# A grouped-query attention block with a K/V cache: part of wo on four DMA engines, sums on VectorE, and division after the turn to tokens

## The chip, the cores and the metric

The kernel runs on one core of one Trainium2 chip. The metric is device microseconds of one execution. Before the change the runs took 187.44, 187.71 and 189.12 us, median 187.71. One execution was also recorded by the hardware profiler: 187.35 us, with a span of 185.6 us from its first to its last instruction.

## The reference

B = 8 sequences with 4 new tokens each, D = 512, 32 query heads, 8 K/V heads (4 query heads share one), 2048 cached keys, head size 128, all bf16.

```python
q = (x @ wq).reshape(B, Sq, Hq, Dh).transpose(0, 2, 1, 3)
k = jnp.repeat(k_cache, rep, axis=1)
v = jnp.repeat(v_cache, rep, axis=1)
scores = jnp.einsum("bhqd,bhkd->bhqk", q, k) * (Dh ** -0.5)
p = softmax(scores, axis=-1)
o = jnp.einsum("bhqk,bhkd->bhqd", p, v)
return o.transpose(0, 2, 1, 3).reshape(B, Sq, Hq * Dh) @ wo
```

k_cache and v_cache are 33.6 MB each, wq and wo 4.2 MB each: 75.5 MB are read for 32 KB of output.

## The kernel before, in words

The work is cut into 16 units: one sequence b and four of the eight K/V heads (a half hq). A unit has one K tile and one V tile of 2 MB, 128 rows of 16 KB (four heads by 32 stretches of 64 keys). Three K and three V tiles fit (`KB, VB`). The main loop (L327) runs n = 1 to 17: in step n TensorE turns unit n's K, makes unit n-1's scores and unit n-2's V products. Inside a step the order is written out by hand, and each engine runs its instructions in this order; semaphores between engines follow from the tiles.

- `transpose_part` (L144): a quarter of a K tile. TensorE turns eight 128 x 128 blocks (two bf16 taken as one fp32), four to a PSUM buffer `kp` of one bank out of three; VectorE (DVE) copies each four to `kt` (L155).
- `scores` (L213): 16 matmuls into two `s_ps` buffers; ScalarE (ACT) takes the exponential of each into `s_sb` and adds up the rows on the way (`accum_out`, L230).
- `probs_to_keys` (L237): TensorE turns the exponentials so that keys are in rows (`pt`, one PSUM buffer); ACT copies them in eight copies of 32 x 512 to `probs` (L249), one of two buffers.
- `norms` (L256): the row sums are spread by a product on DVE (L258), added over the four groups of rows by a matmul with ones (L265), and DVE takes the reciprocal (L273). Once a unit.
- `values` (L277): 64 matmuls add V's products into `o_ps` (one PSUM buffer); `finish` (L290): DVE multiplies by the reciprocals and writes `oT` in bf16.
- `to_tokens`, `to_wo_rows` (L299, L307): after the eight units of a half, TensorE turns `oT` so that the 64 rows are tokens, DVE copies, TensorE turns again so that rows are rows of wo, DVE copies to `oP`.
- `project` (L316): 16 matmuls for each quarter p of wo's rows, two for each r, into `out_ps`. Quarter 0 stands in step 17 ahead of the last unit's V products, quarters 1 to 3 at the end.

At the start come K0, wq and x, the turn of K0, and q, which is laid out in `q_bd` by DVE and ACT in turn (L202).

All loads are issued by SyncE (SP), in one order: K0, wq, x, K1, K2, V0, K3, V1 and so on, K15, V13, quarter 0 of wo, V14, V15, then quarters 1, 2, and 3 in two parts (6 and 2 of the 8 r's), then four small loads of x into `spare`, of 5, 7, 1 and 3 rows. A load waits for its buffer, and for the load eight before it, since eight semaphores are used in turn. The two stores are issued by ACT and SP.

Of the kernel before, what the change touches and what calls it, by code (L numbers as in the profile page):

```python
# [14 lines left out]
def kernel(  # L15
# [35 lines left out]

    const = ctx.enter_context(tc.tile_pool(name="const", bufs=1))
# [5 lines left out]
    psum_k = ctx.enter_context(tc.tile_pool(name="psum_k", bufs=3, space=bass.MemoryType.PSUM))  # L58
# [3 lines left out]
    psum_l = ctx.enter_context(tc.tile_pool(name="psum_l", bufs=1, space=bass.MemoryType.PSUM))  # L62
# [6 lines left out]
    probs = [const.tile([128, C, G, HQ], BF16, name=f"probs{i}") for i in range(2)]  # L69
    ident = const.tile([128, 128], BF16, name="ident")  # L70
    ident4 = const.tile([128, 128], FP32, name="ident4")
    ones = const.tile([128, 128], FP32, name="ones")
    by_hq = const.tile([128, 2, HQ], FP32, name="by_hq")
    oT = [const.tile([128, HP, 2, B, Sq], BF16, name=f"oT{n}") for n in range(2)]
# [3 lines left out]
    spare = const.tile([16, 4, 32], BF16, name="spare")  # L78
# [5 lines left out]

    def load_k(u):
        hq, b = units[u]
        ks[u] = kpool.tile([128, C, Dh], BF16, tag="k_sb", name="k_sb")
        nc.sync.dma_start(
            ks[u][:, :, :],
            k_cache[b, G * hq : G * hq + G].rearrange("g (s c) d -> (g s) c d", c=C),  # L90
        )

    def load_v(u):
        hq, b = units[u]
        vs[u] = vpool.tile([128, C, Dh], BF16, tag="v_sb", name="v_sb")
        rows = v_cache[b, G * hq : G * hq + G].rearrange("g (s c) d -> (g s) c d", c=C)
        nc.sync.dma_start(vs[u][:, :, :], rows)

    def load_wo(p, r0, n):
        rows = wo[p * HP * 128 : (p + 1) * HP * 128, :].rearrange("(q r) j -> q r j", r=WR)  # L100
        nc.sync.dma_start(wo_sb[:, p, r0 : r0 + n, :], rows[:, r0 : r0 + n, :])  # L101

    load_k(0)
# [3 lines left out]
    for u in range(2, NU + 2):  # L107
        if u < NU:
            loads.append(("k", u))
        if u == NU:  # L110
            loads.append(("w", 0))
        loads.append(("v", u - 2))
    loads.reverse()

    def load_ready(nk, nv):

        while loads:
            kind, u = loads[-1]
            if kind == "w":
                load_wo(u, 0, WR)  # L120
            elif u >= (nk + KB if kind == "k" else nv + VB):
                return
            else:
                (load_k if kind == "k" else load_v)(u)
            loads.pop()
# [6 lines left out]
    nc.gpsimd.memset(probs[0][:, :, :, :], 0.0)  # L132
    nc.gpsimd.memset(probs[1][:, :, :, :], 0.0)  # L133
    nc.gpsimd.memset(ones[:, :], 1.0)
    nc.vector.tensor_reduce(
        out=by_hq[:, :, :],
        in_=ident4[:, :].rearrange("p (z c q) -> p z q c", z=2, q=HQ),
        axis=AX,
        op=ADD,
# [4 lines left out]
    def transpose_part(u, t):  # L144
# [4 lines left out]
        for half in range(2):  # L149
            j0 = t % 2 * J + half * J // 2  # L150
            kp = psum_k.tile([128, J // 2, 128], FP32, tag="k", name="kp")
            for j in range(J // 2):
                w = (t * J + half * J // 2 + j) * 128
                nc.tensor.transpose(kp[:, j, :], k4[:, w : w + 128], ident4[:, :])  # L154
            nc.vector.tensor_copy(  # L155
                out=kt[(u, t // 2)][:, j0 : j0 + J // 2, :, :].rearrange("k j s e -> k (j s e)"),
                in_=kp[:, :, :].rearrange("k j s -> k (j s)").bitcast(BF16),
            )
# [52 lines left out]
    l_sbs = {}  # L211

    def scores(u):  # L213
# [3 lines left out]
        l_sbs[u] = small.tile([128, 2], FP32, tag="l_sb", name="l_sb")  # L217
        for y in range(2):
            s_ps = psum_s.tile([128, 2 * J, S], FP32, tag="s", name="s_ps")
            for e in range(2):  # L220
# [13 lines left out]
                accum_out=l_sbs[u][:, y : y + 1],  # L234
            )

    def probs_to_keys(u):  # L237
# [7 lines left out]
        pr = probs[u % 2][:, :, :, :].rearrange("s (x i k w) g q -> s x g i k w q", x=2, k=4, w=2)  # L245
        for x in range(2):
            for g in range(G):
                z, y = g // 2, g % 2
                nc.scalar.copy(  # L249
                    out=pr[g * S : (g + 1) * S, x, g, :, :, :, :],  # L250
                    in_=halves[(2 * x + y) * S : (2 * x + y + 1) * S, z, :, :, :, :],
                )

    r_sbs = {}

    def norms(u):  # L256
        by_gq = small.tile([128, 2, 2, HQ], FP32, tag="by_gq", name="by_gq")
        nc.vector.tensor_tensor(  # L258
            out=by_gq[:, :, :, :],
            in0=l_sbs[u][:, :].unsqueeze(1).unsqueeze(3).to_broadcast([128, 2, 2, HQ]),  # L260
            in1=by_hq[:, :, :].unsqueeze(2).to_broadcast([128, 2, 2, HQ]),
            op=MULT,
        )
        l_ps = psum_l.tile([128, NQ], FP32, tag="l", name="l_ps")
        nc.tensor.matmul(  # L265
            l_ps[:, :],
            lhsT=ones[:, :],
            rhs=by_gq[:, :, :, :].rearrange("k z y q -> k (z y q)"),
            start=True,
            stop=True,  # L270
        )
        r_sbs[u] = small.tile([128, NQ], FP32, tag="r_sb", name="r_sb")
        nc.vector.reciprocal(r_sbs[u][:, :], l_ps[:, :])  # L273
# [3 lines left out]
    def values(u, half):  # L277
        if half == 0:
            o_pss[u] = psum_o.tile([128, NQ], FP32, tag="o", name="o_ps")
        for i in range(half * C // 2, (half + 1) * C // 2):  # L280
# [4 lines left out]
                rhs=probs[u % 2][:, i, :, :].rearrange("s g q -> s (g q)"),  # L285
# [4 lines left out]
    def finish(u):  # L290
        hq, b = units[u]
        nc.vector.tensor_tensor(  # L292
            out=oT[hq][:, :, :, b, :].rearrange("d h p s -> d p h s"),
            in0=o_pss[u][:, :].rearrange("d (p h s) -> d p h s", p=2, h=HP),
            in1=r_sbs[u][:, :].rearrange("d (p h s) -> d p h s", p=2, h=HP),
            op=MULT,
        )

    def to_tokens(n):  # L299
        nat = psum_l.tile([2 * T, HP, 128], BF16, tag="l", name="nat")  # L300
        for h in range(HP):
            nc.tensor.transpose(
                nat[:, h, :], oT[n][:, h, :, :, :].rearrange("d p b s -> d (p b s)"), ident[:, :]
            )
        nc.vector.tensor_copy(out=nat_sb[:, :], in_=nat[:, :, :].rearrange("t h d -> t (h d)"))

    def to_wo_rows(n):  # L307
        perm = psum_l.tile([128, WR, 2, T], BF16, tag="l", name="perm")
        by_row = nat_sb[:, :].rearrange("t (q r) -> t r q", r=WR)
        for r in range(WR):  # L310
            nc.tensor.transpose(
                perm[:, r, :, :].rearrange("q p t -> q (p t)"), by_row[:, r, :], ident[: 2 * T, : 2 * T]
            )
        nc.vector.tensor_copy(out=oP[n][:, :, :, :], in_=perm[:, :, :, :])

    def project(p, r0, n):  # L316
        for r in range(r0, r0 + n):
            for half in range(2):
                nc.tensor.matmul(  # L319
                    out_ps[half * T : (half + 1) * T, :],  # L320
                    lhsT=oP[p // 2][:, r, p % 2, :],
                    rhs=wo_sb[:, p, r, half * DH : (half + 1) * DH],
                    start=(p == 0 and r == 0),
                    stop=(p == NP - 1 and r == WR - 1),
                )

    for n in range(1, NU + 2):  # L327
# [7 lines left out]
        if w >= 0:  # L335
            norms(w)
        if n < NU:
            transpose_part(n, 2)
        if n == NU - 1:
            probs_to_keys(n - 1)  # L340
        if n == NU + 1:
# [65 lines left out]
```

## Time and profile before

| | |
|---|---|
| runs | 187.44, 187.71, 189.12 us |
| profiled execution | 187.35 us, span 185.6 us |
| TensorE (PE) busy | 137.2 us, 74% |
| VectorE (DVE) busy | 103.6 us, 56% |
| ScalarE (ACT) busy | 102.2 us, 55% |
| DMA | 75.86 MB, mean 409 GB/s over the span |
| chain that ended last | DMA 68%, PE 22%, DVE 4% |
| K and V loads | 16 of 2048 KB each; from issue to landing 21.6 and 25.1 us in the median |

How to read it: the page lists busy time of each engine, the span in 40 slices with the busy share in tenths, the DMA queues, the chain of work that ended last, and the groups of instructions by source line, with the mean of one in ns and the idle time before them. In the time-ordered list each row has its start and its length in us from the span's start, the engine, the line, the operation, the output and input tiles, the count of instructions merged in the row, and in square brackets the idle time before it and what ended that. In a row by stretches, the four pairs are busy us and instruction counts of PE, PEld (weight loads), DVE and ACT, then POOL, then the granted clock, the DMA share and GB/s.

### The profile page before, as it was taken

Reading aid. Unit: us, or ns where it says so; the run is one execution under the profiler, and the core shown is the slowest. Engines: PE = TensorE matmul, PEld = TensorE weight load, DVE = VectorE, ACT = ScalarE, POOL = GpSimd, SP = SyncE. Lnnn points to the kernel's source line nnn. Section 1 sums busy time; section 2 is a strip of 40 time slices with the busy share of each in tenths; the row PEclk is TensorE's granted clock in tenths of the full one; section 3 lists DMA queues with packets and bytes.
Section 4 is the critical chain, followed back from the end, with each engine's and each line's share of the span. In section 5 each row is a group of like instructions: output and inputs, shape, how many; then the busy total and the mean of one; then the engine's idle time right before and its main releaser. Section 6 shows DMA issues by size and latency. Waiting matters only on the chain.

```text
span 185.6 us, 4659 instructions
## 1 busy us (share of the span) xinstructions
PE 137.2 (74%) x2036; PEld 113.4 (61%) x2036; DVE 103.6 (56%) x189; ACT 102.2 (55%) x200; POOL 8.2 (4%) x11
## 2 busy tenths in 40 slices
PE   0092869797978777777777869579777777795872
PEld 0192347595866665757575849377666757585651
DVE  4074188777765747475665756466747475661220
ACT  2000153969576666574839292927566574878700
POOL 8900000000000000000000000000000000000000
PEclk9999589999999999999999999999999999999999
DMA  6998999999999999999999999999999999999970
GB/s 187 484 438 378 434 424 431 434 420 431 438 422 431 422 438 410 441 431 424 434 427 431 434 417 431 441 413 438 424 434 434 417 443 420 417 443 411 417 297 8
DMA packets 5668, 75.86 MB, mean 409 GB/s; under 512 B 688, under 2 KB 784, under 8 KB 1040
## 3 DMA queue, kind: packets, MB, share of 16 engines
q1 hardware_dynamic: 5600, 75.55, 95.9%
q8 instruction: 16, 0.26, 0.5%
q14 instruction: 4, 0.03, 0.0%
q10 hardware_dynamic: 48, 0.02, 0.0%
HBM read 75.53 MB, written 0.03 MB: 407 GB/s over the span
## 4 chain that ended last, share of the span: by engine, by line
DMA 68%; PE 22%; DVE 4%; issue 1%; ACT 1%; SPq 1%
DMA k_sb<-in_k_cache_dram 46%; DMA wo_sb<-in_wo_dram 13%; PE kp L154 12%; DMA x_sb<-in_x_dram 9%; DVE kt L155 3%; PE s_ps L223 3%; PE o_ps L282 3%; PE psq L177 2%; PE l_ps L265 1%; ACT q_bd L202 1%; PE out_ps L319 1%; SPq L101 0%; PE pt L242 0%; DVE by_gq L258 0%; DVE q_bd L202 0%
## 5 line engine op out<-in xcount | busy, mean ns | idle before, releaser
L155 DVE COPY kt<-kp 128x1024 bf16<-128x1024 bf16 x128 | 82.0, 683 | 42.7 <-PE kp L154 42.7
L249 ACT COPY probs<-pt 32x512 bf16<-32x512 bf16 x128 | 73.7, 576 | 49.5 <-PE pt L242 46.7
L154 PE MATMUL kp<-ident,k_sb 128*128 128x128 f32 x512 | 70.6, 284 | 20.2 <-DMA k_sb<-in_k_cache_dram 11.2
L154 PEld LDWEIGHTS kp<-ident,k_sb 128*128 128x128 f32 x512 | 58.3, 147 | 28.8 <-DVE oT L292 9.7
L282 PE MATMUL o_ps<-probs,v_sb 128*128 128x64 bf16 x1024 | 34.8, 194 | 0.2 <-DMA v_sb<-in_v_cache_dram 0.2
L282 PEld LDWEIGHTS <-v_sb 128*128 128x128 bf16 x1024 | 33.9, 98 | 0.8 <-DMA v_sb<-in_v_cache_dram 0.5
L230 ACT ACTIVATE s_sb<-s_ps 128x512 bf16<-128x512 f32 x32 | 22.6, 734 | 1.3 <-PE s_ps L223 0.9
L265 PE MATMUL l_ps<-by_gq,ones 128*128 128x64 f32 x32 | 6.9, 298 | 15.6 <-DVE by_gq L258 15.6
L223 PE MATMUL s_ps<-kt,q_bd 128*32 128x512 bf16 x256 | 17.5, 390 | 0.0
L265 PEld LDWEIGHTS l_ps<-by_gq,ones 128*128 128x128 f32 x32 | 4.8, 188 | 19.5 <-DVE by_gq L258 17.7
L273 DVE RECIPROCAL r_sb<-l_ps 128x64 f32<-128x64 f32 x16 | 8.9, 558 | 9.1 <-PE l_ps L265 9.1
L186 ACT ACTIVATE q_nat<-psq 128x512 bf16<-128x512 f32 x2 | 1.2, 597 | 20.4 <-PE psq L177 20.4
L242 PE MATMUL pt<-ident,s_sb 128*128 128x128 f32 x64 | 9.7, 274 | 2.1 <-ACT s_sb L230 2.1
L292 DVE TENSOR_TENSOR oT<-o_ps,r_sb 128x64 bf16<-128x64 f32 x16 | 3.6, 225 | 13.6 <-PE o_ps L282 13.5
L223 PEld LDWEIGHTS <-q_bd 128*32 128x32 bf16 x256 | 5.6, 94 | 6.1 <-issue 2.5
L242 PEld LDWEIGHTS pt<-ident,s_sb 128*128 128x128 f32 x64 | 7.4, 141 | 2.3 <-ACT s_sb L230 2.3
L230 ACT ACTIVATION_READ_ACCUMULATOR s_sb<-s_ps 128x1 f32 x32 | 6.0, 188 | 0.0
L319 PE MATMUL out_ps<-wo_sb,oP 128*32 128x256 bf16 x64 | 4.2, 273 | 1.1 <-DMA wo_sb<-in_wo_dram 0.6
L374 ACT CAST out_sb<-out_ps 64x256 bf16<-64x256 f32 x1 | 0.4, 365 | 6.9 <-PE out_ps L319 6.9
L319 PEld LDWEIGHTS <-oP 128*32 128x32 bf16 x64 | 3.0, 96 | 1.7 <-issue 0.7
L177 PE MATMUL psq<-wq_sb,xT_sb 128*32 128x512 bf16 x32 | 3.6, 631 | 0.3 <-DVE xT_sb L170 0.3
L133 POOL MEMSET probs<- 128x4096 bf16 x1 | 3.5, 3512 | 0.0
(27 smaller groups left out, 29.9 us busy)
## 6 DMA issues: line engine op xcount, KB each, us to landing
k_sb<-in_k_cache_dram SPq DMA_DIRECT2D x16, 2048.0 KB, 21.6
v_sb<-in_v_cache_dram SPq DMA_DIRECT2D x16, 2048.0 KB, 25.1
wq_sb<-in_wq_dram SPq DMA_DIRECT2D x1, 4096.0 KB
wo_sb<-in_wo_dram SPq DMA_DIRECT2D x3, 1024.0 KB, 20.9
wo_sb<-in_wo_dram SPq DMA_DIRECT2D x1, 768.0 KB, 23.2
wo_sb<-in_wo_dram SPq DMA_DIRECT2D x1, 256.0 KB, 23.4
x_sb<-in_x_dram SPq DMA_DIRECT2D x1, 32.0 KB
spare<-in_x_dram SPq DMA_DIRECT2D x1, 0.3 KB
```

Source lines behind the costliest of these rows:

```text
L154: nc.tensor.transpose(kp[:, j, :], k4[:, w : w + 128], ident4[:, :])
L155: nc.vector.tensor_copy(out=kt[(u, t // 2)][:, j0 : j0 + J // 2, :, :].rearrange("k j s e -> k (j s e)"), in_=kp[:, :, :].rearrange("k j s ...
L177: nc.tensor.matmul(psq[g * T : (g + 1) * T, :], lhsT=xT_sb[:, r, :], rhs=wq_sb[:, r, c0 : c0 + rep * Dh], start=(r == 0), stop=(r == R - 1),)
L223: nc.tensor.matmul(s_ps[m * 32 : (m + 1) * 32, :, :], lhsT=q_bd[:, hq, e, g, b, :, :], rhs=kt[(u, th)][:, :, g * S : (g + 1) * S, e], star ...
L230: nc.scalar.activation(out=s_sbs[u][:, :, y, :, :].rearrange("r j s w -> r j w s"), in_=s_ps[:, :, :].rearrange("r (j w) s -> r j w s", w= ...
L242: nc.tensor.transpose(pt[:, i, :], s4[:, i * 128 : (i + 1) * 128], ident4[:, :])
L249: nc.scalar.copy(out=pr[g * S : (g + 1) * S, x, g, :, :, :, :], in_=halves[(2 * x + y) * S : (2 * x + y + 1) * S, z, :, :, :, :],)
L265: nc.tensor.matmul(l_ps[:, :], lhsT=ones[:, :], rhs=by_gq[:, :, :, :].rearrange("k z y q -> k (z y q)"), start=True, stop=True,)
L273: nc.vector.reciprocal(r_sbs[u][:, :], l_ps[:, :])
L282: nc.tensor.matmul(o_pss[u][:, :], lhsT=vs[u][:, 2 * (th * 2 * J + 2 * (2 * j + x) + w) + c, :], rhs=probs[u % 2][:, i, :, :].rearrange("s ...
L292: nc.vector.tensor_tensor(out=oT[hq][:, :, :, b, :].rearrange("d h p s -> d p h s"), in0=o_pss[u][:, :].rearrange("d (p h s) -> d p h s", ...
L319: nc.tensor.matmul(out_ps[half * T : (half + 1) * T, :], lhsT=oP[p // 2][:, r, p % 2, :], rhs=wo_sb[:, p, r, half * DH : (half + 1) * DH], ...
```

## The change

- **wo.** The first 128 rows of quarters 0 and 1 (256 rows) go to a tile `wo_e` of 48 partitions (rows 0 to 15 and 32 to 47 filled, the rest zero) by eight loads of four rows of 8 KB each, which stand after V2 to V9 in the order of loads. The other 896 rows of both quarters come in one load after V15, with seven r's instead of eight, then quarter 2, then quarter 3 in two equal parts. Quarter 0 no longer stands ahead of V14. The `spare` loads are gone. Loads and stores together are 48 (45 before).
- **Projection.** All of it stands at the end: 16 matmuls for `wo_e`, 14 for each of quarters 0 and 1, then 16 for each of quarters 2 and 3; before, 16 stood ahead of the last V products and 48 behind.
- **Sums.** ACT's exponentials add up nothing; DVE adds each unit's `s_sb` (1024 columns) by one reduction into `l_sb` (`add_up`). Once in a half, `sums` spreads them (two products on POOL), adds them by two small matmuls and takes 64 x 8 reciprocals.
- **Division.** `finish` copies `o_ps` to `oT` in fp32; the division is made in `to_tokens`, with tokens in rows, four heads at a time: four steps in all, two in each half, the turned outputs in a `kp` buffer. The small results (`l_ps`, `perm`) use the buffer of the V products; the pool `psum_l` is gone. In the first half these steps are spread over n = 10 to 13.
- **K.** `kp` has two banks and two buffers: eight blocks are turned, then DVE copies 128 x 2048 in one instruction.
- **probs.** Four buffers instead of two (half a unit each); of a unit's eight copies DVE makes the first one (even units) or two (odd units), ACT the rest, group by group.

The core of the diff:

```diff
-    psum_k = ctx.enter_context(tc.tile_pool(name="psum_k", bufs=3, space=bass.MemoryType.PSUM))
+    psum_k = ctx.enter_context(tc.tile_pool(name="psum_k", bufs=2, space=bass.MemoryType.PSUM))
...
-    psum_l = ctx.enter_context(tc.tile_pool(name="psum_l", bufs=1, space=bass.MemoryType.PSUM))
...
+    def load_wo_e(i):
+
+        p0, k0 = i // 4 * 32 + i % 4, i // 4 * HP * 128
+        rows = wo[k0 : k0 + 16 * WR, :].rearrange("(q r) j -> q r j", r=WR)
+        nc.sync.dma_start(wo_e[p0 : p0 + 13 : 4, :, :], rows[i % 4 : i % 4 + 13 : 4, :, :])
...
+    nc.gpsimd.memset(wo_e[:, :, :], 0.0)
     load_k(0)
...
-        if u == NU:
-            loads.append(("w", 0))
         loads.append(("v", u - 2))
+        if 4 <= u < 12:
+            loads.append(("e", u - 4))
...
-        for half in range(2):
-            j0 = t % 2 * J + half * J // 2
-            kp = psum_k.tile([128, J // 2, 128], FP32, tag="k", name="kp")
...
+        kp = psum_k.tile([128, J, 128], FP32, tag="k", name="kp")
+        for j in range(J):
+            w = (t * J + j) * 128
+            nc.tensor.transpose(kp[:, j, :], k4[:, w : w + 128], ident4[:, :])
...
-                accum_out=l_sbs[u][:, y : y + 1],
-            )
+            )
+
+    def add_up(u):
+        hq, b = units[u]
+        nc.vector.tensor_reduce(
+            out=l_sb[hq][:, b, :],
+            in_=s_sbs[u][:, :, :, :, :].rearrange("r j y s w -> r y j (s w)"),
+            axis=mybir.AxisListType.XY,
+            op=ADD,
+        )
...
+        for g in range(G):
+            for x in range(2):
+                pr = probs[u % 2 * 2 + x][:, :, :, :].rearrange("s (i k w) g q -> s g i k w q", k=4, w=2)
                 z, y = g // 2, g % 2
-                nc.scalar.copy(
-                    out=pr[g * S : (g + 1) * S, x, g, :, :, :, :],
+                (nc.vector.tensor_copy if g == 0 and x <= u % 2 else nc.scalar.copy)(
+                    out=pr[g * S : (g + 1) * S, g, :, :, :, :],
                     in_=halves[(2 * x + y) * S : (2 * x + y + 1) * S, z, :, :, :, :],
                 )
...
+        add_up(u)
...
     def finish(u):
         hq, b = units[u]
+        nc.vector.tensor_copy(
+            out=oT[hq][:, :, :, b, :].rearrange("d h p s -> d p h s"),
+            in_=o_pss[u][:, :].rearrange("d (p h s) -> d p h s", p=2, h=HP),
+        )
...
+    def sums(n):
+
+        by_tok = small.tile([128, 2, 2, B, Sq], FP32, tag="by_tok", name="by_tok")
...
+        l_ps = psum_o.tile([2 * T, 2, rep], FP32, tag="o", name="l_ps")
...
+    def to_tokens(n, h0):
+        nat = psum_k.tile([2 * T, 4, 128], FP32, tag="k", name="nat")
...
         nc.vector.tensor_tensor(
+            out=nat_sb[:, h0 * 128 : (h0 + 4) * 128].rearrange("t (h d) -> t h d", h=4),
+            in0=nat[:, :, :],
+            in1=r_sbs[n][:, h0 : h0 + 4].unsqueeze(2).to_broadcast([2 * T, 4, 128]),
             op=MULT,
         )
...
         if w == B:
-            to_tokens(0)
-        if w == B + 1:
+            sums(0)
+        if w in (B, B + 1):
+            to_tokens(0, (w - B) * 4)
+        if w == B + 2:
             to_wo_rows(0)
+        if w == B + 3:
+            to_extra_rows()
         load_ready(min(n + 1, NU), max(w + 1, 0))
...
-            for p, r0, k in [(1, 0, 8), (2, 0, 8), (3, 0, 6), (3, 6, 2)]:
-                load_wo(p, r0, k)
-            for i, k in enumerate([5, 7, 1, 3]):
-                nc.sync.dma_start(spare[:k, i, :], x.flatten_outer_dims()[:k, :32])
-
-    to_tokens(1)
-    project(1, 0, WR)
-    to_wo_rows(1)
-    project(2, 0, WR)
-    for r in range(0, WR, 2):
-        project(3, r, 2)
+            load_wo(0, 0, WM)
+            load_wo(2, 0, WR)
+            for r in (0, 4):
+                load_wo(3, r, 4)
+
+    out_ps = psum_s.tile([2 * T, DH], FP32, tag="s", name="out_ps")
+    sums(1)
+    to_tokens(1, 0)
+    to_tokens(1, 4)
+    for r in range(WR):
+        project(wo_e[:, r], oE[:, r, :], first=r == 0)
+    for p in range(NP):
+        if p == 2:
+            to_wo_rows(1)
+        for r in range(WM if p < 2 else WR):
+            project(wo_sb[:, p, r], oP[p // 2][:, r, p % 2, :], last=p == NP - 1 and r == WR - 1)
```

## The prediction

> **What bounds the kernel now.** I read the page first (which resource is full), then the stretches of the steady part (how full), then the time-ordered list of instructions from the last K tile to the end (which wait ends last there), then the trace's own packet and semaphore records for the sixteen DMA engines. Page and stretches:
>
> ```profile
> span 185.6 us, 4659 instructions
> ...
> DMA  6998999999999999999999999999999999999970
> ...
> q8 instruction: 16, 0.26, 0.5%
> ...
> L155 DVE COPY kt<-kp 128x1024 bf16<-128x1024 bf16 x128 | 82.0, 683 | 42.7 <-PE kp L154 42.7
> L249 ACT COPY probs<-pt 32x512 bf16<-32x512 bf16 x128 | 73.7, 576 | 49.5 <-PE pt L242 46.7
> ```
>
> ```profile
> 60.00:80.00 20.00, 15.84 (x249) 12.97 (x241) 12.41 (x23) 12.93 (x26) 0.00 (x0) 1.00 1.01 431
> 140.00:157.00 17.00, 12.99 (x212) 11.40 (x210) 10.62 (x20) 9.79 (x21) 0.00 (x0) 1.00 1.01 428
> ```
>
> The DMA engines are full from the third slice to the last but one; at 431 GB/s a 2 MB tile takes 4.87 us, a unit (K and V) 9.73, a 1 MB part of wo 2.43. No compute engine is full. The end is another stage; in the time-ordered list:
>
> ```profile
> 154.71 0.60 PE L242 MATMUL pt<-ident,s_sb 128*128 128x128 f32 x4
> 155.40 4.78 ACT L249 COPY probs<-pt 32x512 bf16<-32x512 bf16 x8 [3.56 <-PE pt L242]
> 157.23 1.06 PE L154 MATMUL kp<-ident,k_sb 128*128 128x128 f32 x8 [0.98 <-DMA k_sb<-in_k_cache_dram]
> 160.21 0.73 ACT L230 ACTIVATE s_sb<-s_ps 128x512 bf16<-128x512 f32 x1
> ```
>
> ```profile
> 163.22 4.78 ACT L249 COPY probs<-pt 32x512 bf16<-32x512 bf16 x8 [1.57 <-PE pt L242]
> ...
> 168.03 0.73 ACT L230 ACTIVATE s_sb<-s_ps 128x512 bf16<-128x512 f32 x1
> ...
> 170.28 4.78 ACT L249 COPY probs<-pt 32x512 bf16<-32x512 bf16 x8 [0.80 <-PE pt L242]
> ...
> 174.14 2.06 PE L282 MATMUL o_ps<-probs,v_sb 128*128 128x64 bf16 x64 [0.22 <-DMA v_sb<-in_v_cache_dram]
> 176.24 0.23 DVE L292 TENSOR_TENSOR oT<-o_ps,r_sb 128x64 bf16<-128x64 f32 x1 [2.71 <-PE o_ps L282]
> ...
> 178.79 0.42 DVE L314 COPY oP<-perm 128x512 bf16<-128x512 bf16 x1 [0.92 <-PE perm L311]
> ...
> 180.89 1.05 PE L319 MATMUL out_ps<-wo_sb,oP 128*32 128x256 bf16 x16 [0.56 <-DMA wo_sb<-in_wo_dram]
> 181.97 0.36 ACT L374 CAST out_sb<-out_ps 64x256 bf16<-64x256 f32 x1 [6.92 <-PE out_ps L319]
> ```
>
> From 155.4 ScalarE runs copies, exponentials, copies without rest to 175.06; at 174.14 the last V tile lets the last V products start; at 180.89 the last wo part lets the last projection start; TensorE ends at 181.95. So the end has two chains, the data and ScalarE's, within a microsecond of each other.
>
> The semaphore records show why the data ends at 181.48 there: the sixteen increments of the last wo transfer run from 178.19 to 181.48 (mean 180.0). In the packet records a 16 KB packet takes 0.607 us on an engine, and each of the sixteen 16 KB instruction fetches of q8 holds up one engine by about 1 to 1.5 us; they go round eight engines, twice. The spare transfers (5, 7, 1, 3 rows, one engine a row from the lowest) tell the low engines: engine 0 ends at 178.41, engines 1 and 2 at 178.78 and 179.80 (which is which is not seen), 3 and 4 at 178.20 and 180.19.
>
> **The change, part by part.** The sum is made against the profiled execution: 187.35 us, span 185.6 (0.36 below the median of 187.71).
>
> 1. *256 rows on engines 0 to 3.* 64 KB more for each of the four: 64/16 x 0.607 = 2.43 us; 16 KB less for all sixteen: 0.61. The twelve others end at 181.48 - 0.61 = 180.87; the four at 180.2, 180.6, 181.6 and, for engine 3, 180.0 or 182.0. So the data ends at 181.6 to 182.0, no earlier. Off that: ACT and DVE have two 8 KB fetches each in the trace (51.6, 60.0, 150.3, 158.8; about 0.6 to 0.85 us each time on the engine hit), and with fewer instructions each gets one; the two slow low engines gain that. Data end 180.9 to 181.4. The eight small transfers: the trace's x_sb, 32 KB too, lands 0.16 us after wq_sb's last increment, so no fixed cost behind a full queue. (The Trainium skill, DMA: Bandwidth & Descriptors, section Bandwidth, says that transfers under 64 KB are descriptor-dominated and lists 0.95 us for 64 KB; by that eight would cost some 7 us and the kernel would be near 194. The row is a measurement behind a full queue, which is this case.)
>
> 2. *wo behind V.* Before, 1 MB of wo stood ahead of the last two V tiles; now all of it follows. V15 lands 2.43 us earlier, 171.7 (the four engines: 171.0 to 172.0).
>
> 3. *K turns in two banks.* DVE copies of 1024 columns take 683 ns, and rows of 512 (0.42) and 1024 (0.68) give 0.15 fixed and 0.26 per 512: 1.21 for 2048, so 4.84 per unit for 5.46. But the copy now begins after eight turns, not four.
>
> 4. *DVE takes 1 or 2 of 8 probs copies.* DVE's cost is not in the trace: between 0.42 (the packed 512 of oP) and 0.68 (q_bd's first, unpacked 512); the new copy reads every second element, so 0.62. The order of the built kernel shows that ScalarE's first copy of a unit waits for DVE's last, since both read one PSUM bank. The trace has that wait already:
>
> ```profile
> 24.25 2.46 DVE L202 CAST q_bd<-pse 64x512 bf16<-64x512 f32 x4
> ...
> 24.95 2.37 ACT L202 CAST q_bd<-pse 64x512 bf16<-64x512 f32 x4 [1.35 <-DVE q_bd L202]
> ```
>
> DVE's copy in turn stands behind DVE's 1.21 us K copy. So ScalarE saves 0.6 or 1.2 us of copies and starts later by about as much: the balance is nearly zero. This is where I think the change loses its gain.
>
> 5. *Sums on DVE.* One reduction of 1024 (128 elements took 0.24: 0.11 + 8 x 0.133 = 1.17 us) per unit; gone are by_gq, reciprocal (0.56), the l_ps matmuls with their wait (1.08 on TensorE per unit) and ScalarE's accumulator reads. An exponential falls from 0.73 toward the 0.60 of q_nat's 512: 0.65.
>
> 6. *Steady part: nothing.* Per unit DVE has 4.84 + 0.93 + 1.17 + 0.23 = 7.2, ScalarE 5.2, TensorE 7.0; the longest cycle (K copy, probs copies, ScalarE, next exponential, next turn) is about 7.8, against 9.73 of data. Cover: a K tile is issued 21.6 us before it lands, so two units of delay would have to pile up. The sums and turns of the first half (n = 9 to 13, about 1 us of TensorE each) hide there too. At the start, POOL's wo_e memset (3.51, as 128x4096) puts the identity at about 5, still before K0 (TensorE starts at 8.84); the third pse buffer is missed for about 0.6, while K4's issue has 10 us in hand.
>
> 7. *The end, scheduled by these rows.* K14 and K15 land as before (147.4, 157.1). Unit 13's turn ends at 154.7 (V12 lands at 152.2, then 0.94 + 0.95 + 0.6); DVE's K copy ends 155.5, its two probs copies 156.7; ScalarE's six copies (0.597 each) 160.35; exponentials 161.7; turn 162.35; DVE copy 163.0; seven copies 167.25; DVE's reduction and two K copies end 166.55, so the last scores are ready; exponentials 168.6; turn 169.25; two DVE copies 170.5; five ScalarE copies, 173.55. **The last V products start at 173.6**, not at V15's landing. Then in order on TensorE: 64 products 1.91, DVE copy with both hand-overs 0.48, sums 0.5 (two l_ps pairs 0.44), eight fp32 turns 0.94, 16 + 28 projections (0.066 each) 2.86, turn 0.64, DVE copy with hand-overs 0.64, 32 projections 2.07: 10.04. End 183.65, against 181.95: +1.7. Behind it nothing changes (copy, two stores, end). All wo parts have landed by 181.4, so the last projections wait for nothing. Sum: 187.35 + 1.7 = **189.05, say 189.1**; 0.7% over the median.
>
> Ends of the unknowns: probs copy 0.42 or 0.68: five of them stand in the chain, -1.0 or +0.3. Exponential 0.60 or 0.73: four, -0.2 or +0.3. Sums and fp32 turns: 0.3 either way. If the K copy is not 1.21 but 2 x 0.683, +0.15 each for two. Together 187.5 to 190.2.
>
> **Rivals.** *A, not slower.* ScalarE's chain is not late, because fewer copies count and the wait on DVE costs little; the products start as V15 lands, 171.8, TensorE ends at 181.85 and the time is 187.25, with 0.3 either way for its end. It decides if the chain is ready before 172. For: ScalarE has 20 us less work in all. Against: the two waits above, and even then 0.1 is gained against the profiled 187.35. *B, DVE becomes the bound of the end.* The reduction (1.17 by extension from 128 elements) stands in front of the last unit's two K copies. If it takes 2.2 us the last scores come 1 us later; with a probs copy of 0.68, 190.4. For: no row has such a reduction. Against: only the end counts. *C, the four engines overshoot.* If engine 3 is the slow one and the 8 KB fetches stay, the last wo part lands at 182.0; its eight matmuls end at 182.5, 187.9 if the chain were early, and hidden at 183.65. *D, the balance is not as described:* the fetches fall elsewhere, and one of the four gets one: 1.2 more, 183.2, still just hidden.
>
> **How the numbers follow.** Main case 0.50 (188.4 to 189.9), A 0.20, B 0.23, C and D 0.07. One per cent, 1.9 us, is about what a measurement of this kernel can tell from no change: the bounds are 185.8 and 189.6. Of the main case about a quarter lies over 189.6, B all; C and D and most of A within; below 185.8 only what no row here shows, 0.05 taken from A. So faster 0.05, same 0.55, slower 0.40. The range, 187.0 to 190.8, leaves out A's low end and B's high one.
>
> **What would show it.** Right: the last V products wait for ACT probs and start near 173.6; the 16 + 16 last projections run without a DMA wait and end near 183.6; V15 in at about 171.8; DVE's probs copy near 0.62 us; K14 and K15 at 147 and 157. Wrong: these products start at a DMA landing (A); DVE's reduction over 1.5 us (B); the last out_ps group waits for wo_sb (C, D); or a steady unit over 9.8 us, which nothing above has.

## The result: 193.4 us, and the profile after

The changed kernel takes 193.43 us in the median (193.13, 193.24 and 193.61; one disturbed execution is left out, as such ones are in the runs below, except that e1 and e4 are given whole), the kernel before 187.59: a ratio of 1.029 (95% interval 1.023 to 1.035). Forecast were 189.1 and a range from 187.0 to 190.8. So it is slower, the side on which the 189.1 stood (the forecast gave "same" 0.55 and "slower" 0.40), but by 5.8 us where 1.7 were worked out against the profile.

The page of the profiled execution (193.61 us), the lines that answer to those of before; PEclk is the granted clock of TensorE in tenths over 40 slices:

```profile
span 191.6 us, 4570 instructions
...
PEclk9999766999999999889999999699999999998569
DMA  6999999999999999999999999999999999999400
...
L178 DVE COPY kt<-kp 128x2048 bf16<-128x2048 bf16 x64 | 76.8, 1220 | 35.3 <-PE kp L177 34.9
L278 ACT COPY probs<-pt 32x512 bf16<-32x512 bf16 x104 | 59.9, 576 | 62.6 <-DVE probs L278 60.4
...
L259 DVE TENSOR_REDUCE l_sb<-s_sb 128x2 f32<-128x1024 bf16 x16 | 19.1, 1197 | 0.0
L278 DVE COPY probs<-pt 32x512 bf16<-32x512 bf16 x24 | 16.2, 675 | 4.3 <-PE pt L271 4.1
```

The same clock line of the kernel before:

```profile
PEclk9999589999999999999999999999999999999999
```

The single operations cost what was predicted (1.220 for 1.21, 1.197 for 1.17, 0.675 for 0.62), and ScalarE's copies now wait for VectorE's (60.4 us in all), as predicted. The DMA is full up to the last three of the 40 slices, before up to the last two: the data is not late, something behind it is. New is the clock line: in the last slices TensorE got half its clock. The time-ordered list from unit 13's copies to the end:

```profile
156.03 1.39 DVE L278 COPY probs<-pt 32x512 bf16<-32x512 bf16 x2
...
157.53 3.58 ACT L278 COPY probs<-pt 32x512 bf16<-32x512 bf16 x6 [4.54 <-DVE probs L278]
...
170.23 1.40 DVE L278 COPY probs<-pt 32x512 bf16<-32x512 bf16 x2 [2.84 <-PE pt L271]
...
171.74 3.58 ACT L278 COPY probs<-pt 32x512 bf16<-32x512 bf16 x6 [2.25 <-DVE probs L278]
...
174.77 3.11 PE L291 MATMUL o_ps<-probs,v_sb 128*128 128x64 bf16 x64 [2.71 <-ACT probs L278]
...
182.44 3.17 PE L368 MATMUL out_ps<-wo_sb,oP 128*32 128x256 bf16 x28
...
186.74 1.93 PE L368 MATMUL out_ps<-wo_sb,oP 128*32 128x256 bf16 x32 [0.52 <-DVE oP L359]
```

The chain is the predicted one, and the last V products wait for ScalarE (2.71 us), not for V15, which landed at 172.04. But the 64 products take 3.11 us (2.06 before) and 28 projections 3.17, while 32 projections at the end take only 1.93. The stretches of the profile show why (columns as before: PE, PEld, DVE, ACT, POOL, granted clock, DMA share, GB/s):

```profile
171.94:175.35 3.41, 0.70 (x26) 0.68 (x22) 1.04 (x2) 3.25 (x6) 0.54 (x2) 1.00 1.01 426
175.35:185.59 10.24, 9.83 (x107) 7.19 (x104) 1.79 (x4) 0.00 (x0) 0.00 (x0) 0.50 0.42 169
185.59:189.00 3.41, 2.56 (x42) 2.04 (x40) 0.42 (x1) 0.29 (x1) 0.00 (x0) 1.00 0.00 0
```

In 3.41 us TensorE works 0.70; for the next 10.24 us, with TensorE busy for 9.83 of them, the granted clock is 0.50. In the kernel before the clock stayed at 1.0 from 24.5 us to the end of the work. Only one of the three executions has a trace; the mean granted clock of the other two, 0.946 and 0.927, is near its 0.929 (the profiled execution of before: 0.980).

The two profiled executions in parts, with run e14 (below: the change at full clock) as the third column:

| us | before | after | e14 |
|---|---|---|---|
| start of the last V products | 174.14 | 174.77 | 174.68 |
| from there to TensorE's end | 7.80 | 13.90 | 9.46 |
| TensorE's end to the last instruction | 3.63 | 2.93 | 2.93 |
| outside the span | 1.78 | 2.01 | 1.92 |
| time | 187.35 | 193.61 | 188.99 |

Of the 6.26 us between the first two columns, 0.63 are a later start, 1.66 (9.46 - 7.80) more work behind it, 4.44 (13.90 - 9.46) half clock, and -0.70 + 0.23 the rest.

### The profile page after: what moved, and what is told of

It reads as the page before. It is cut to its first block, busy times and chain, and to the rows that moved or that the text cites. A ratio compares the mean times of both kernels' runs of the same rounds, so it can differ in the third digit from the quotient of the medians.

```text
span 191.6 us, 4570 instructions
## 1 busy us (share of the span) xinstructions
PE 143.2 (75%) x2031; PEld 116.5 (61%) x2031; DVE 123.2 (64%) x140; ACT 86.7 (45%) x144; POOL 12.9 (7%) x18
## 4 chain that ended last, share of the span: by engine, by line
PE 37%; DMA 33%; DVE 14%; ACT 12%; issue 2%; SPq 0%; ACTq 0%; DVEq 0%
PE kp L177 16%; DMA v_sb<-in_v_cache_dram 14%; DMA k_sb<-in_k_cache_dram 11%; ACT probs L278 9%; DMA x_sb<-in_x_dram 9%; PE o_ps L291 7%; DVE kt L178 5%; DVE probs L278 5%; PE s_ps L244 4%; PE out_ps L368 4%; DVE l_sb L259 2%; PE psq L200 2%; PE nat L333 1%; ACT s_sb L251 1%; PE pt L271 1%
## 5 line engine op out<-in xcount | busy, mean ns | idle before, releaser
L178 DVE COPY kt<-kp 128x2048 bf16<-128x2048 bf16 x64 | 76.8, 1220 | 35.3 <-PE kp L177 34.9
L278 ACT COPY probs<-pt 32x512 bf16<-32x512 bf16 x104 | 59.9, 576 | 62.6 <-DVE probs L278 60.4
L177 PEld LDWEIGHTS kp<-ident,k_sb 128*128 128x128 f32 x512 | 59.8, 149 | 31.7 <-issue 9.5
L244 PE MATMUL s_ps<-kt,q_bd 128*32 128x512 bf16 x256 | 20.0, 427 | 0.2 <-DVE kt L178 0.2
L259 DVE TENSOR_REDUCE l_sb<-s_sb 128x2 f32<-128x1024 bf16 x16 | 19.1, 1197 | 0.0
L278 DVE COPY probs<-pt 32x512 bf16<-32x512 bf16 x24 | 16.2, 675 | 4.3 <-PE pt L271 4.1
L152 POOL MEMSET probs<- 128x2048 bf16 x4 | 7.0, 1804 | 0.0
L301 DVE COPY oT<-o_ps 128x64 f32<-128x64 f32 x16 | 3.4, 215 | 5.2 <-PE o_ps L291 4.9
L349 PE MATMUL perm<-ident,nat_sb 64*128 64x64 bf16 (+1 forms) x23 | 1.6, 209 | 4.4 <-DVE oT L301 4.4
L349 PEld LDWEIGHTS <-nat_sb 64*128 64x128 bf16 (+1 forms) x23 | 1.5, 138 | 4.8 <-issue 4.7
```

The lines of the kernel that those rows point to most:

```text
L152: nc.gpsimd.memset(probs[i][:, :, :, :], 0.0)
L178: nc.vector.tensor_copy(out=kt[(u, t // 2)][:, t % 2 * J : (t % 2 + 1) * J, :, :].rearrange("k j s e -> k (j s e)"), in_=kp[:, :, :].rearr ...
L244: nc.tensor.matmul(s_ps[m * 32 : (m + 1) * 32, :, :], lhsT=q_bd[:, hq, e, g, b, :, :], rhs=kt[(u, th)][:, :, g * S : (g + 1) * S, e], star ...
L259: nc.vector.tensor_reduce(out=l_sb[hq][:, b, :], in_=s_sbs[u][:, :, :, :, :].rearrange("r j y s w -> r y j (s w)"), axis=mybir.AxisListTyp ...
L278: (nc.vector.tensor_copy if g == 0 and x <= u % 2 else nc.scalar.copy)(out=pr[g * S : (g + 1) * S, g, :, :, :, :], in_=halves[(2 * x + y) ...
L301: nc.vector.tensor_copy(out=oT[hq][:, :, :, b, :].rearrange("d h p s -> d p h s"), in_=o_pss[u][:, :].rearrange("d (p h s) -> d p h s", p= ...
```

## The experiments

The theory at the start: the late chain leaves TensorE idle, the idle stretch lets its clock fall, and the tail, made longer by the change, runs at half speed. Rivals: the tail is long in itself, or the late start is the whole loss. Ratios are to the kernel before on the same chip. The idle turns in some runs are transposes of the identity, results unused.

**e1, idle turns ahead of the last V products.**

```diff
+        if n == NU + 1:
+            fp = psum_k.tile([128, J, 128], FP32, tag="k", name="fp")
+            for j in range(16):
+                nc.tensor.transpose(fp[:, j % J, :], ident4[:, :], ident4[:, :])
         if w >= 0:
             values(w, 0)
```

> The changed kernel (193.4 us) with sixteen 128x128 fp32 turns of the identity added on TensorE between the V products of unit 14 and those of unit 15, results unused (about 2.1 us of the 2.71 us in which TensorE waited for ScalarE's copies). Theory (the idle stretch lets the granted clock fall to 0.5 for the whole tail): clock 1.0 through the tail, last V products still start near 174.8, 64 of them take 2.06, TensorE ends about 3.9 us earlier, 189.5 us. Rival 'the tail is long in itself' (the clock costs nothing that the order of work does not): 193.4 or a little more, the turns being extra work. Rival 'the late start': 193.4 as well.

Three executions took 194.5 to 194.7, one 188.81. The profiled one (194.54) has clock 1.0 in the tail, and there TensorE needs 9.46 us from the products' start to its end, as the theory says. But half clock came earlier: in its clock records it begins at 99.3, 119.8, 140.3, 150.5 and 164.2, and the last products start at 180.13, 5.4 us late. The data is not the reason: K15 lands at 157.42 and the last wo part at 181.23, as in the change (157.44 and 181.25). So the tail's part was right, and the place of the cure wrong: the same kernel has several rests, and which of them meets the clock differs between executions (the mean clock was 0.91 to 0.92 in the three long ones, 0.963 in the short one).

**e2, all copies from pt on ScalarE, half by half, as before the change.**

```diff
-        for g in range(G):
-            for x in range(2):
+        for x in range(2):
+            for g in range(G):
...
-                (nc.vector.tensor_copy if g == 0 and x <= u % 2 else nc.scalar.copy)(
+                nc.scalar.copy(
```

> The changed kernel with the copies from pt as they were before: all eight on ScalarE, the four of the first half of the keys ahead of the four of the second. Nothing else is undone. Theory: the first half of the last V products starts at V15's landing, about 172.0, the second when the copies end, about 174.1, so 1.5 to 2 us of the late start go; but TensorE still rests for 2.5 us and more ahead of it, so the clock still falls to 0.5 and the tail still runs at half speed: 191.0 to 192. Rival 'the late start is all': 188.5 or less, with the clock at 1.0. Rival 'the tail is long in itself': over 192.5.

187.39 profiled, ratio 0.998 (0.995 to 1.001): the whole loss is gone, with wo, sums, K turns and the longer tail as in the change. The clock stayed at 1.0 from 32.6 us on. I had expected it to fall; it did not, since the first half of the products went at V15's landing and the rest ahead of it was only 1.27 us:

```profile
172.08 1.11 PE L291 MATMUL o_ps<-probs,v_sb 128*128 128x64 bf16 x32 [1.27 <-DMA v_sb<-in_v_cache_dram]
...
174.16 1.09 PE L291 MATMUL o_ps<-probs,v_sb 128*128 128x64 bf16 x32 [0.97 <-ACT probs L278]
```

**e3, both.** The two edits of e1 and e2 together (`fill(16)` here and below stands for e1's loop, with 16 turns):

```diff
+        if n == NU + 1:
+            fill(16)
...
+                nc.scalar.copy(
```

> Both of the foregoing: ScalarE makes all copies from pt, and the sixteen idle turns stand ahead of the last V products. Theory: the two effects add, first half of the products at about 172.0 to 172.3 and clock 1.0 to the end: 187.0 to 188.2, level with the kernel before (187.6). Rival 'the tail is long in itself': not under 190. If the turns hold up the products, the products start a little after 172.3 and the time is up to 0.5 us more.

187.32 profiled, 0.999 (0.994 to 1.003). Nothing is left for the idle turns to save, and they cost nothing.

**e4, the projections of the 256 rows ahead of the last products.**

```diff
+        if n == NU + 1:
+            out_ps = psum_s.tile([2 * T, DH], FP32, tag="s", name="out_ps")
+            for r in range(WR):
+                project(wo_e[:, r], oE[:, r, :], first=r == 0)
         if w >= 0:
             values(w, 0)
...
-    out_ps = psum_s.tile([2 * T, DH], FP32, tag="s", name="out_ps")
...
-    for r in range(WR):
-        project(wo_e[:, r], oE[:, r, :], first=r == 0)
```

> The changed kernel with the sixteen projections of the 256 wo rows (all there since about unit 10) moved from behind the last V products to ahead of them, into TensorE's rest. No work is added. Theory: about 1.05 us of the rest is filled, TensorE is busy for about half of the 3.41 us stretch instead of a fifth, which is near the point at which the clock of the other stretches stayed up (0.48 and more stayed at 1.0, 0.46 and less fell): if it stays, 188.5; if it falls, 193.4 less the 1.9 us that these projections took at half clock, 191.5. Rival 'the tail is long in itself': 192.3 (1.05 less), whatever the clock.

190.75 to 194.96. In the profiled execution (194.65) half clock begins at 138.4, 152.0 and 165.7, and the products start at 181.31. It misses both numbers, for e1's reason.

**e5, VectorE's copies kept, ScalarE's half by half.**

```diff
-        for g in range(G):
-            for x in range(2):
+        for g, x in [(0, 0), (0, 1), (1, 0), (2, 0), (3, 0), (1, 1), (2, 1), (3, 1)]:
```

> The changed kernel with VectorE's copies kept, but ScalarE's in the order of the halves of the keys (groups 1 to 3 of the first half, then of the second), so that the last V products can start two ScalarE copies earlier. Theory now (the copies on VectorE are the loss: ScalarE stands behind VectorE's queue, the chain comes late, and TensorE's rests let the clock fall): little is undone, first half of the products at 173.5 and the second at 175.3, so 188.5 to 189.5 if the clock stays up in the tail and 191 to 194 in executions where it falls. Rival 'the order of the copies is the loss': 187.4, as with all copies on ScalarE in that order (187.4 in the run e2).

192.8 to 194.8, ratio 1.032 (1.022 to 1.042). The order alone cures nothing; the rival falls.

**e6 and e7, all copies on ScalarE but group by group, without and with idle turns.** e6 takes VectorE's copies away and leaves the order (first hunk); e7 has e1's sixteen turns as well (second).

```diff
-                (nc.vector.tensor_copy if g == 0 and x <= u % 2 else nc.scalar.copy)(
+                nc.scalar.copy(
...
+        if n == NU + 1:
+            fill(16)
```

> The changed kernel with all eight copies on ScalarE, but group by group as in the change: the first half of the last V products waits for the seventh copy. No copy on VectorE. Theory 'VectorE's copies are the loss': the chain is as early as in e2 up to the last copies, the products start at about 173.5 for 172.08 and end 0.5 later: 187.9 while the clock stays up. But TensorE then rests from 170.8 to 173.5, as long as in the changed kernel (2.7 us); if such a rest alone lets the clock fall, the tail costs 3 to 4 us more: 191 to 192. Rival 'the order of the copies is the loss': 191 or more with the clock at 1.0.

> e6 with sixteen idle turns (1.95 us of TensorE) in the rest ahead of the last V products, results unused. Against e6 this shows what the rest costs through the clock alone: both have the same chain. Theory 'a rest of 2.7 us lets the clock fall': e7 stays at 1.0, 187.9, and e6 is 3 to 4 us slower in the executions whose rest falls into one stretch of 3.41 us. Rival 'the clock follows something else': e6 and e7 agree within 0.5 us.

e6: 188.9 to 189.0 in four executions, 187.65 and 187.68 in two, ratio 1.005 (1.002 to 1.007). e7: 187.4 to 187.7 in five, 189.0 in one, ratio 0.9995 (0.997 to 1.002). In both the last products start within 0.1 us of 173.6. The stretches around that start, first of e6, then of e7:

```profile
169.55:172.96 3.41, 1.28 (x44) 1.26 (x41) 0.23 (x1) 3.26 (x7) 0.55 (x2) 1.00 0.97 408
172.96:176.37 3.41, 2.81 (x54) 2.80 (x54) 0.00 (x0) 1.13 (x2) 0.00 (x0) 0.50 1.02 424
```

```profile
168.99:172.41 3.42, 3.42 (x79) 3.42 (x76) 0.72 (x2) 2.97 (x6) 0.55 (x2) 1.00 0.97 411
172.41:175.82 3.41, 2.21 (x66) 1.91 (x64) 0.21 (x1) 1.64 (x3) 0.00 (x0) 1.00 1.01 419
```

One edit, work that nobody needs, and the clock of the next stretch is 1.0 instead of 0.50: the kernel with more work is 1.2 us faster in the median. That the rest lets the clock fall is shown; the size is a third of the expected 3 to 4 us, because here half clock lasted one stretch of 3.41 us, in the change three.

**e8, VectorE's copies put into the kernel before.** 
```diff
-        for x in range(2):
-            for g in range(G):
+        for g in range(G):
+            for x in range(2):
                 z, y = g // 2, g % 2
-                nc.scalar.copy(
+                (nc.vector.tensor_copy if g == 0 and x <= u % 2 else nc.scalar.copy)(
```

> The kernel before with one part of the change alone: of each unit's eight copies from pt VectorE makes the first (even units) or the first two (odd units), group by group as in the change. wo, sums, K turns and the tail are as before. Theory 'VectorE's copies are the loss': ScalarE's copies stand behind VectorE's queue here too, the last V products start 1 to 2 us after 174.14, 188.5 to 190, and up to 193 where TensorE's rest lets the clock fall. Rival 'the loss needs the long tail and wo behind V': 187.4 to 188.2, since the products wait for V15 until 174.1 anyway.

187.5 to 188.1 in four executions, 189.1 and 189.5 in two; ratio 1.002 (0.998 to 1.007). Not slower: my theory then, "VectorE's copies are the loss", is too short. In the kernel before V15 lands at 174.1 and the products cannot start sooner; in the change V15 lands at 172.0. That the same delay therefore lies open only in the change, with more work behind it, is argued and not shown: the one profiled execution of e8 took 193.77 us and is none of these six.

**e9, sums on ScalarE again.**

```diff
                 func=EXP,
+                accum_out=l_sb[hq][:, b, y : y + 1],
             )
...
-        add_up(u)
```

> The changed kernel with the sums taken by ScalarE's exponentials again (accum_out, as before the change), so that VectorE's reduction of 1.20 us a unit is gone. VectorE's copies from pt stay. Theory (VectorE's queue holds K copy, probs copies, reduction and oT copy in a row, and TensorE waits for the oT copy at its end: 2.70 us at 116.5, 2.61 at 136.6): these two rests fall to about 1.4, the stretches of half clock in the steady part go, the last products start about 173.5, and the time is 188.5 to 189.5 where the clock stays up in the tail. Rival 'VectorE's probs copies alone are the loss': 192.5 or more still, since the copies and ScalarE's wait for them are as in the change.

The two rests for the oT copy fell as expected, from 2.70 and 2.61 to 1.58 and 1.49, but the time is 191.7 to 194.2 (1.029, 1.021 to 1.037), on the rival's side in two of three executions. In the profiled execution (194.23) the data came later than in the change, K15 at 161.08 for 157.44: its slices from 19 to 53 us have 382 to 402 GB/s, those of the change 424 to 434. What slowed the data is not settled, so the time says nothing on the sums. The rest ahead of the last products stayed at 2.71 us, and half clock followed it.

**e10, the reduction behind the oT copy.**

```diff
-        add_up(u)
...
             values(w, 1)
             finish(w)
+        if n <= NU:
+            add_up(n - 1)
```

> The changed kernel with the reduction moved behind the oT copy on VectorE's queue (and so, in the step that turns the last K tile, behind its K copies as well). No work is added or taken away. Theory 'the order on VectorE's queue': like the run with the sums on ScalarE, 188.5 to 189.5 where the clock stays up, and no rest of TensorE over 2 us in the steady part. Rival 'VectorE's probs copies alone': 192.5 or more.

190.3 to 191.7, ratio 1.017 (1.009 to 1.025), between the theory's 188.5 to 189.5 and the rival's 192.5. Against the change's 1.029 (1.023 to 1.035) some 40% of the loss go by order alone, though the two intervals just meet. The wait behind it, in the changed kernel at unit 10:

```profile
116.31 1.37 DVE L278 COPY probs<-pt 32x512 bf16<-32x512 bf16 x2
...
117.61 1.20 DVE L259 TENSOR_REDUCE l_sb<-s_sb 128x2 f32<-128x1024 bf16 x1
...
118.83 0.22 DVE L301 COPY oT<-o_ps 128x64 f32<-128x64 f32 x1
119.20 0.37 PE L320 MATMUL l_ps<-by_h,by_tok 128*64 128x4 f32 x4 [2.70 <-DVE oT L301]
```

The result of the V products shares its buffer with `l_ps` and `perm`, so TensorE stands until VectorE's queue has come to the oT copy, behind two copies and the reduction. In e10 this rest is 1.58 us, and half clock after 100 us comes only in the tail, for one stretch.

**e11, all rests filled.** 8, 12 or 16 idle turns at the start of each step from 5 on, ahead of the first half's sums and turns, of unit 14's turn, and of the last products. `fill(k)` is that loop with k turns.

```diff
+        if 5 <= n < NU:
+            fill(8)
         if n < NU:
             transpose_part(n, 0)
...
         if n == NU - 1:
+            fill(8)
             probs_to_keys(n - 1)
...
+        if n == NU + 1:
+            fill(16)
         if w >= 0:
             values(w, 0)
...
+        if w in (B, B + 2, B + 3):
+            fill(12)
         if w == B:
             sums(0)
```

> The changed kernel with idle fp32 turns (8, 12 or 16 of 0.13 us each, results unused) ahead of every point at which TensorE rested over 1.8 us: at the start of each step from 5 on, ahead of the turns of the first half's outputs, of unit 14's exponentials and of the last V products. Every dependency and every other instruction is as in the change. Theory (a stretch of 3.41 us in which TensorE is busy for less than 0.46 to 0.48 is followed by half clock, which is most of the loss): the clock stays at 1.0 after the start, and the time is that of the plain chain, 188.5 to 189.5 (the prediction's 189.05; the one undisturbed execution of e1 took 188.81). Rival 'the late chain itself costs the 6 us': 193 or more, with the clock at 1.0.

191.0 in two executions, 193.7 in a third; ratio 1.022 (1.013 to 1.030). The clock is 1.0 from 30.4 us to the end of the work and the tail takes 9.46 us, but the turns delay the chain: the last products start at 176.64, 1.87 later than in the change. The number is missed, by 1.5 us, for a reason that the trace shows.

**e12, a version to beat both.** e2, and the following:

```diff
+        if n == NU + 1:
+            sums(1)
+            out_ps = psum_s.tile([2 * T, DH], FP32, tag="s", name="out_ps")
+            for r in range(WR):
+                project(wo_e[:, r], oE[:, r, :], first=r == 0)
         if w >= 0:
             values(w, 0)
...
-        if p == 2:
+        if p == 1:
             to_wo_rows(1)
...
-            for r in (0, 4):
-                load_wo(3, r, 4)
+            for r, k in ((0, 6), (6, 2)):
+                load_wo(3, r, k)
```

> A version to beat both: the run e2 (all copies on ScalarE, halves in order; 187.39 profiled) with the last sums and the projections of the 256 rows ahead of the last V products, the turn of the second half's outputs between the projections of quarters 0 and 1 instead of behind both, and the last quarter loaded as 6 and 2 rows of each partition. The tail behind the last V products loses about 0.4 (sums), 1.05 (projections) and 0.9 (copy behind the turn), but the last wo part lands at 181.3 to 181.7 and four projections of 0.066 follow: TensorE ends near 182.0 for 182.69, so 186.7, 0.3 to 0.4% under the kernel before. Rival 'the data alone sets the end': 187.2 to 187.4, no change from e2.

186.5 to 186.75 in seven executions, as forecast (186.7), ratio 0.993 (0.990 to 0.996): 0.7% faster than the kernel before, and faster than the change. The end is now the data's:

```profile
178.39 1.81 PE L368 MATMUL out_ps<-wo_sb,oP 128*32 128x256 bf16 x30
...
180.87 1.05 PE L368 MATMUL out_ps<-wo_sb,oP 128*32 128x256 bf16 x16 [0.67 <-DMA wo_sb<-in_wo_dram]
```

**e13, e10 with e1's idle turns.** To e10's edit comes:

```diff
+        if n == NU + 1:
+            fill(16)
         if w >= 0:
             values(w, 0)
```

> e10 (the reduction behind the oT copy) with sixteen idle fp32 turns ahead of the last V products, results unused. In e10 the rest of 2.71 us there is the only one in the last 80 us of the run that was followed by half clock (the 64 products took 3.33 for 2.03). Theory (the clock is the part of the loss that the prediction lacked): clock 1.0 in the tail, last products at 174.7, 9.47 us of TensorE behind their start as in e1 and e11, TensorE ends at 184.1 for 185.44 in e10: 189.1, which is what was predicted for the change. Rival 'the late chain itself': 190.3 as in e10.

188.6 to 188.85, ratio 1.005 (1.0035 to 1.007). Against e10 (median 190.5) the filled rest saves 1.7 us. The one profiled execution (194.03) is none of these, but it has clock 1.0 from 31.0 us to the end of the work, and its tail takes 9.46 us for 10.77 in e10.

**e14, the change with four of its rests filled.** e1's sixteen turns, and:

```diff
+        if w in (B, B + 2):
+            fill(10)
+        if w == B + 3:
+            fill(6)
         if w == B:
             sums(0)
```

> The changed kernel with idle turns in four of its rests alone: ten ahead of the two waits of 2.6 to 2.7 us for the oT copy (116.5 and 136.6), six ahead of the wait of 1.8 us at 146.9, sixteen ahead of the last V products. Unlike e11 nothing is put ahead of a K turn, where the idle turns delayed the chain (last products at 176.64 there). Theory: no stretch of half clock from 100 us on, last products at 174.8 to 175.2, 189.2 to 189.6. Rival 'the late chain itself': 193.

188.9 to 189.2, median 188.99, ratio 1.0065 (1.005 to 1.008). Every dependency is the change's, and its last products start at the same place (174.68 for 174.77):

```profile
171.81 1.94 PE L393 MATMUL fp<-ident 128*128 128x128 f32 x16
...
174.68 2.03 PE L291 MATMUL o_ps<-probs,v_sb 128*128 128x64 bf16 x64 [0.93 <-ACT probs L278]
...
182.21 1.92 PE L368 MATMUL out_ps<-wo_sb,oP 128*32 128x256 bf16 x32 [0.52 <-DVE oP L359]
```

So the change at full clock costs 0.65%, and half clock 193.43 - 188.99 = 4.4 us, 2.3%; in the two profiles it is the 4.44 us of the tail, since the start differs by 0.09. "The late chain costs the 6 us" falls.

**e15, the kernel before with 48 transfers.**

```diff
-            for i, k in enumerate([5, 7, 1, 3]):
+            for i, k in enumerate([5, 7, 1, 3, 1, 1, 1]):
```

> The kernel before with three more small loads of x, so that loads and stores together are 48 as in the change, and the two stores fall on the last two of the eight semaphores that are used in turn. From the landing of the last store to the last instruction the kernel before takes 1.65 us, the changed one and e2 0.9: SyncE waits at the end for the eight in turn, and the stores were among the first of them. Theory: 0.6 to 0.7 us less, 186.7 to 187.0. Rival 'the end depends on something else, such as an instruction fetch, that falls where it falls': 187.3 to 187.5, no change. If SyncE's queue holds the store up behind the new loads: 0.1 to 0.5 more.

188.7, ratio 1.005 (1.004 to 1.006): slower, a miss. From the last store's landing to the last instruction it took 1.4 us (before 1.6, after 0.9), but its data is later: the last projections waited for wo until 182.50 (180.89 before), and why three small loads do that is not settled. Why the end became shorter stays open too.

## Why the prediction was wrong, step by step

- *Steps 1 and 2, the data:* right. The last wo part landed at 181.25 (180.9 to 181.4 predicted), V15 at 172.04 (171.7), K15 at 157.44 (157.1). The eight loads of 32 KB cost nothing that can be seen there.
- *Steps 3 to 5, the prices:* right, 1.220, 0.675 (near the upper end), 1.197, a pair of exponentials 1.32 for 1.30 (one still takes 0.738, but the second begins 0.60 after the first, without the accumulator's read between them). That ScalarE stands behind VectorE, and that this eats the gain, was right.
- *Step 6, "steady part: nothing":* right for the data, and in the changed kernel it cost little. But it overlooked that TensorE waits for the oT copy at the end of VectorE's queue, twice for 2.6 to 2.7 us, and what such a rest does to the clock. In e1, e4 and e5 these and other rests, with half clock behind them, moved the last products to 179 to 181.
- *Step 7, the end:* here it failed, in the term "10.04 us of TensorE work" behind the last products. It measured 13.90. At full clock it is 9.46 (e14), so the counting was even 0.6 too dear; 4.44 are the granted clock, of which no step spoke. The start, 173.6, was 1.2 too early (1.1 by e14): unit 13's turn ended at 155.29 for 154.7, and the copies, exponentials and their hand-overs took 0.5 more than the rows taken.
- *"Behind it nothing changes":* wrong by 0.7 in the kernel's favour.
- *Readings of the lines:* ScalarE does not run "without rest" from 155.4: the prediction's own lines show it waiting for TensorE's turns for 1.57 us ahead of 163.22 and 0.80 ahead of 170.28. The sum goes step by step and does not use it.
- *The sum:* without the clock the change takes 188.99, and 189.05 was worked out; but that is three errors which cancel (+1.1, -0.6, -0.7, and +0.1 outside the span), not four right terms.
- *The rivals:* A, B, C and D all failed: the products did not start at V15, the reduction was no dearer, wo landed in time. None of the signs named for them appeared, and the time was wrong all the same. The case that came, a rest of TensorE that halves its clock, was not among them, so the range could not reach it. The prediction's own schedule held it: it left TensorE without work from the end of unit 14's products to 173.6, and the clock line of before shows half clock behind a rest at the start.

## What to carry to other kernels

A change that makes TensorE wait costs the wait and then, perhaps, half speed for 3.4 to 10 us: ask of each new rest how much TensorE works in the 3.41 us around it, and put work that is ready there (e12 has the last sums and 16 projections) rather than behind it. Handing part of a row of copies to a second engine gained nothing here, where both read one buffer in turn, and it put those copies into that engine's queue, ahead of what TensorE waits for. Moving a load forward pays only if the chain that uses it can follow.

## What the runs showed of the hardware

The clock follows a fixed grid of 3.413 us. I took TensorE's busy share in every such stretch behind 30 us, in all 17 profiled executions, where the clock was 1.0:

| busy share of the stretch | stretches | followed by half clock |
|---|---|---|
| under 0.455 | 15 | 15 |
| 0.455 to 0.485 | 20 | 9 |
| over 0.485 | 694 | 0 |

The kernel before had one stretch of 0.48 and one of 0.50 and stood close to the edge. The Trainium skill (TensorE: Matmul & The Clock Gate, section What's actually happening) gives the window, 3413 ns and free-running, which agrees; it says that the clock falls after at least one idle window, and its section Why this matters for your kernels warns of rests over about 3 us. Here that is too mild: rests of 1.8 to 2.7 us were enough, in stretches in which TensorE worked for almost half of the time. Since the grid is not tied to the kernel, the same rest may meet one stretch or be split over two: the rest of 2.61 us that ends at 139.2 lies in one stretch in e1 (busy 0.33, then half clock), and over two in the change (0.64 and 0.60, and the clock stayed at 1.0). This would also explain that e6 took both 187.65 and 188.9, but only an execution of 189.0 was profiled there.

How long half clock lasts is not explained: of 30 stretches at half clock 24 were followed by full clock, 22 of them with TensorE busy for 0.97 and more, two with 0.82 and 0.88; the changed kernel's tail stayed at half behind one of 0.88 and one of 1.00.
